# Block products for the first feed-forward matmul from chunk 7 instead of 15, accumulated in two PSUM banks

## The chip, the cores and the metric

The kernel runs on one core of a Trainium2 chip, with nothing running on the other cores. The metric is the time of one execution on the device in microseconds (us), from the first to the last instruction and what the launch adds around them. A core has five engines that each work through a queue of their own: TensorE (PE in the profile, its weight loads PEld), VectorE (DVE), ScalarE (ACT), GpSimd (POOL) and SyncE (SP), which here issues all DMAs. Matrix products land in PSUM, which has eight banks; everything else works from SBUF.

## The reference

The first half is a linear attention with random features, the second a feed-forward layer on its output:

```python
q_s, k_s = q * scale, k * scale                  # batch 8, heads 8, 576 tokens, head size 64
phi(x) = exp(x @ omega.T - |x|^2/2 - max) / sqrt(128)      # 128 features
kv  = sum over tokens of phi(k_s) * v            # per batch and head: 128 x 64
z   = sum over tokens of phi(k_s)
attn = (phi(q_s) @ kv) / (phi(q_s) @ z + 1e-6)
x = attn as 4608 tokens x 512
h = x @ w_in                                     # 512 -> 2048
g = h * tanh(softplus(h))                        # Mish
out = g @ w_out                                  # 2048 -> 512, float32
```

## The kernel before

**Precision.** Each float32 operand of a large product is split into two float16 numbers, a high part (a cast) and a low part (the rest). A product is then three TensorE products, low by high, high by low and high by high, summed in one PSUM bank.

**Chunks.** The 4608 tokens are 18 chunks of 256 (`CH`, `NCH`). A k task makes the features of two heads of one batch and its key-value sums; a q task makes the attention output `x` of 128 tokens, splits it (`x_parts`) and sends it transposed to SBUF with a DMA of SP's queue. `ff_in(c)` makes `h` of chunk c, `ff_out(c - 1)` the output of the chunk before. The main loop takes one step of `ff_in` ("i") and one of `ff_out` ("o") in turns, as the string `order` says, and between them one `step()` of an agenda in which the attention's tasks and the work put off with `later(n, ...)` (n steps later) wait for their slot. `pace(c)` sets how far ahead the attention's tasks are begun: the q tasks of a chunk start 1.6 to 2.5 chunks before its `ff_in`. The instructions are traced in this order; a scheduler then places them on the engines' queues in order of that priority as its own cost model sees them ready, and the chip follows the queues as they were placed.

**Plain chunks (2 to 14).** `ff_in(c)` takes eight steps. A step (line 676) fills one bank of the pool `ps_h` (two banks) with 24 matmuls of 256 columns; ACT then applies Mish straight from the bank (`mish`, line 821), and after every second step `g_split` (lines 72 and 83) splits the result. `ff_out` takes eight steps of 12 matmuls of 512 columns (line 845). `order` is "io" eight times.

**Block chunks (15 to 17, from `SC0` on).** `ff_in7(c)` computes the same `h` by a scheme of seven products of half-size blocks instead of eight (Winograd's form of Strassen's): `x` is cut into two halves of its columns and of its tokens, `w_in` into halves of its rows and columns, and seven products of sums of such blocks give the four blocks of `h`. Per chunk there are two groups (`gr`) of 1024 columns of `w_in`, each of seven steps of 24 matmuls of 128 columns (line 779). The sums of `w_in` that the scheme needs (s1 to s4) are made once by `s_make`, four pieces of work on DVE and ACT in chunks 11 to 14, and stored in DRAM. Each use fetches one back with two DMAs of 256 KB (`ask_sum`, line 751) into one of three places of a ring, which takes the room of blocks that are no longer needed; a load is asked for three uses ahead, behind the product that frees its place. The sums of `x` (t1 to t4) are made by `x_sums` for each chunk: four subtractions on DVE (line 548), four splits instead of two, four transposing DMAs instead of two. In this version each product gets a bank of `ps_a` (four banks, which the attention uses too): ACT copies the first into SBUF, and DVE adds every later product into SBUF (seven additions a group, line 788); Mish then reads SBUF.

In SBUF, `h` tiles (tag "ht", `HB` buffers, which `s_make` uses too), `x`'s regions 2 and 3 (tag "vf", shared with the loads of v), and split rows waiting for their transpose (tag "xs", two buffers) matter to the change.

Of the kernel before, what the change touches and what calls it, by code (L numbers as in the profile page):

```python
# [30 lines left out]
def tile_kernel(  # L31
# [19 lines left out]
    NCH = NT * P // CH  # L51
    FG = 8
    FQ = 4
    SC0 = 15
    SCALE = 1.0 / math.sqrt(math.sqrt(D))
    EPS = 1e-6 * M
    D1 = D + 1
# [30 lines left out]
    dve.memset(lnt, LNT)  # L88


    idle = const.tile([P, 512], F16, name="idle")
    dve.memset(idle, 1.0)

    def spin(n, left, right):
# [46 lines left out]

    NB = 8
    BW = KT * DF // NB
    wo_t = const.tile([P, NB, 2, BW], F16, name="wo")
    slots = [const.tile([P, 2, BW], F16, name=f"w{i}") for i in range(NB + 1)]
    slots += [wo_t[:, i] for i in range(NB)]
    def flat32(slot):
        return slot.rearrange("p a b -> p (a b)").bitcast(F32)  # L150

# [355 lines left out]
    def x_region(c, r):  # L507

        n = (4, 4, 4, 2)[r]
        if r < 2:  # L510
            return xT[c].rearrange("p a k s -> p (a k s)")[:, r * 1024:(r + 1) * 1024].rearrange(
                "p (a k s) -> p a k s", a=2, k=n
            )
        if (c, r) not in x_more:
            x_more[c, r] = sb.tile([P, 2, n, P], F16, tag="vf", name=f"xm{c}_{r}", bufs=5)
        return x_more[c, r]

    x_even = {}
# [175 lines left out]

    SUMS = ("s2", "s3", "s1", "s4")
    sums = {}

    def block(sl, a, row):  # L700
# [52 lines left out]
    def ff_in7(c):  # L753

        must(4, "x", c)
        sp = [(b_scales(b), lo, hi) for b, lo, hi in spans(c * CH, CH)]
        right = dict(b11=(0, 0), b21=(0, 2), t3=(1, 0), b22=(1, 2), t1=(2, 0), t2=(2, 2), t4=(3, 0))
        if c == SC0:
            must(4, "sums")
            for _ in range(3):  # L760
                ask_sum()

        def left(gr, op, i, a, k):
            hb, o = i // 2, k * 2 * P + i % 2 * P
            if op in SUMS:
                n = uses.index((c, gr, op))
                assert n < asked[0]
                return ring[2 * (n % 3) + hb][:, a, o:o + P]
            sl = slots[4 * gr + hb + (2 if op == "a22" else 0)]
            o += 0 if op == "a11" else BW // 2  # L770
            return sl[:, a, o:o + P]

        def products(gr, op_l, op_r):
            r, k0 = right[op_r]
            mm = [(a, y, k) for a, y in ((1, 0), (0, 1), (0, 0)) for k in range(2)]
            ph = ps_a.tile([P, FQ, P], F32, tag="a", name=f"p_{op_l}_{c}_{gr}")
            for i in range(FQ):
                for n, (a, y, k) in enumerate(mm):
                    nc.tensor.matmul(  # L779
                        out=ph[:, i, :], lhsT=left(gr, op_l, i, a, k), rhs=x_region(c, r)[:, y, k0 + k, :],  # L780
                        start=n == 0, stop=n == len(mm) - 1,
                    )
            if op_l in SUMS:
                ask_sum()
            return ph

        def add(out, in0, bank):
            dve.tensor_tensor(out=out, in0=bank, in1=in0, op=ALU.add)  # L788

        for gr in range(FT // FG):  # L790
            gT[c, gr] = sb.tile([P, 2, FG, CH], F16, tag="g", name=f"g{c}_{gr}", bufs=GB)
            h = [sb.tile([P, FQ, CH], F32, tag="ht", name=f"h{c}_{gr}_{q}", bufs=HB) for q in range(2)]
            c11, c12, c21, c22 = (x[:, :, o:o + P] for x in h for o in (0, P))


            p1 = products(gr, "a11", "b11")
            cast(act, c21, p1)
            yield
            add(c11, c21, products(gr, "a12", "b21"))
            yield  # L800
            add(c12, c21, products(gr, "s2", "t2"))
            yield
            add(c21, c12, products(gr, "s3", "t3"))
            yield
            p5 = products(gr, "s1", "t1")
            add(c22, c21, p5)
            add(c12, c12, p5)
            yield
            add(c12, c12, products(gr, "s4", "b22"))
            later(1, mish, sp, h[0], h[0])  # L810
            later(2, g_split, c, gr, 0, sp, h[0])
            yield
            add(c21, c21, products(gr, "a22", "t4"))
            later(1, mish, sp, h[1], h[1])
            later(2, g_split, c, gr, 1, sp, h[1])
            yield

    def mish(sp, h, ph):

# [57 lines left out]
        nc.sync.dma_start(out=out[row:row + P, :], in_=o)  # L877


    GB, HB, QB = 4, 5, 1  # L880
    w_dma = nc.sync

    FIRST = (0, 1, 2, 3, 4, 4, 9, 9, 19, 21, 24, 27, 32, 36, 43, 58, 59, 68)
# [45 lines left out]
    def later(after, fn, *args):  # L929
        def gen():  # L930
            fn(*args)
            yield 0
        start(gen(), after)
# [93 lines left out]
        at(slot[0] + 16 * (SC0 - 6) + 2 + 11 * i, lambda i=i: start(s_make(i // 2, i % 2)))  # L1027
    for c in range(2, NCH):
        fi, fo = (ff_in if c < SC0 else ff_in7)(c), ff_out(c - 1)
        order = "io" * 8 if c < SC0 else "iioiioioioi" * 2  # L1030
        for j, what in enumerate(order):
            if j % 2 == 0 and given[0] < min(pace(c + j / len(order)), len(items)):
                give()
            next(fi if what == "i" else fo, None)
            if (j + 1) * 16 // len(order) > j * 16 // len(order):
                step()
        for gen in (fi, fo):
            next(gen, None)
# [47 lines left out]
```

## Time and profile before

| | us |
|---|---|
| median of the runs shown | 969.31 |
| lowest run | 968.18 |
| span of the profiled execution (first to last instruction) | 965.3 |
| PE busy in it | 947.3 |
| ACT busy | 633.5 |
| DVE busy | 624.4 |
| POOL busy | 224.0 |

No time is listed for the profiled execution beside its span; the median of the runs is 4.0 us above that span. Matmuls are pipelined, so a mean duration in the list of groups (380 ns for a matmul of 512 columns) is longer than the step from one matmul to the next; the chain of work and the timeline show how long a run of matmuls takes. A line such as L72 or L83 is that of a helper (`cast`, `rest`) and serves many tiles; the names of the tiles tell which. The chunks are not marked in the trace. Their borders are read off PE's timeline, where a plain chunk is eight runs of 24 matmuls of line 676: chunk 3 starts at 225.3 us, chunk 7 at 422.4, chunk 12 at 667.3, chunk 14 at 771.3, chunk 15 at 820.9, and the last product of chunk 17 ends at 941.0.

### The profile page before, as it was taken

How to read it: one execution, taken by the hardware profiler on the slowest of the kernel's cores; microseconds unless marked ns; L12 is line 12 of the kernel's file. 1: busy time of each engine (PE TensorE's matmuls, PEld its weight loads, DVE VectorE, ACT ScalarE, POOL GpSimd, SP SyncE). 2: the span in 40 equal slices, each digit the busy share in tenths (PEclk: the TensorE clock that was granted, in tenths of full speed). 3: DMA queues.
4: the chain of work that ended last, by engine and by line, in shares of the span. 5: the costliest groups of instructions: out<-in, count | busy, mean ns of one | idle time of the engine just before them, and what ended most of it. 6: DMA issues, size and time to landing. Idle time of an engine off the chain costs nothing. (4 is left out here: it accounts for less than half of the span.)

```text
span 965.3 us, 20405 instructions
## 1 busy us (share of the span) xinstructions
PE 947.3 (98%) x8616; PEld 681.2 (71%) x8616; DVE 624.4 (65%) x1080; ACT 633.5 (66%) x818; POOL 224.0 (23%) x141
## 2 busy tenths in 40 slices
PE   9999989999999999999999999999999999999998
PEld 6788874677777777777777776777766776777773
DVE  5879797596675666656464665788889647633330
ACT  4658875687787777778667775778676866332231
POOL 0000052243233322332233333222231322200000
PEclk9989999999999999999999999999999999999999
DMA  9766324431541445313432263323552155833410
GB/s 290 265 210 205 108 50 91 102 76 54 115 104 39 113 79 117 59 59 78 97 68 60 73 119 64 89 81 74 134 122 72 34 101 102 181 116 123 141 56 33
DMA packets 142411, 100.24 MB, mean 104 GB/s; under 512 B 108656, under 2 KB 121072, under 8 KB 142320
## 3 DMA queue, kind: packets, MB, share of 16 engines
q1 hardware_dynamic: 142320, 98.95, 40.3%
q8 instruction: 67, 1.10, 0.5%
q14 instruction: 24, 0.20, 0.1%
HBM read 58.95 MB, written 13.63 MB: 75 GB/s over the span
## 5 line engine op out<-in xcount | busy, mean ns | idle before, releaser
L845 PE MATMUL po<-wo,g 128*128 128x512 f16 x1632 | 375.0, 380 | 0.0
L676 PE MATMUL ph<-xT,w 128*128 128x256 f16 (+1 forms) x2816 | 345.6, 279 | 0.7 <-ACT xT L72 0.7
L676 PEld LDWEIGHTS <-w 128*128 128x128 f16 x2688 | 261.8, 98 | 48.2 <-issue 0.7
L845 PEld LDWEIGHTS <-g 128*128 128x128 f16 x1632 | 155.1, 98 | 163.9 <-issue 2.0
L83 DVE SCALAR_TENSOR_TENSOR g<-h,us,g 128x1024 f16<-128x1024 f32 (+3 forms) x92 | 118.4, 1298 | 38.0 <-ACT g L72 37.5
L821 ACT ACTIVATE h<-ph,us 128x512 f32<-128x512 f32 (+3 forms) x152 | 83.2, 572 | 80.8 <-PE ph L676 80.1
L81 POOL TENSOR_TENSOR sq<-fq,sq 64x1024 f16<-64x1024 f32 x31 | 69.6, 2245 | 164.7 <-issue 69.0
L81 POOL TENSOR_TENSOR sk<-fk,sk 64x1152 f16<-64x1152 f32 x24 | 60.6, 2523 | 109.1 <-issue 26.3
L81 POOL TENSOR_TENSOR xs<-x,xs 128x512 f16<-128x512 f32 (+1 forms) x35 | 45.3, 1294 | 157.6 <-DVE xs L74 69.7
L72 ACT ACTIVATE g<-h,us 128x1024 f16<-128x1024 f32 (+3 forms) x80 | 72.6, 932 | 1.2
L821 ACT ACT_TABLE_LOAD x55 | 70.6, 1283 | 1.0
L354 ACT ACT_TABLE_LOAD x53 | 68.0, 1283 | 1.0
L339 DVE TENSOR_REDUCE mxq<-pq 128x4 f32<-128x512 f32 x72 | 46.8, 683 | 33.7 <-PE pq L330 33.7
L81 DVE TENSOR_TENSOR qn<-eq,qn 128x1024 f16<-128x1024 f32 x31 | 39.0, 1257 | 37.2 <-ACT qn L72 37.2
L779 PEld LDWEIGHTS <-w 128*128 128x128 f16 x1008 | 58.4, 98 | 5.9
L339 DVE TENSOR_REDUCE mxk<-pk 128x4 f32<-128x512 f32 (+1 forms) x96 | 50.2, 549 | 17.5 <-PE pk L330 17.5
L821 ACT ACTIVATE h<-h,us 128x1024 f32<-128x1024 f32 (+2 forms) x16 | 14.7, 933 | 61.6 <-DVE h L788 61.6
L354 ACT ACTIVATE eq<-eq,lnt 128x1024 f32<-128x1024 f32 x31 | 35.6, 1148 | 27.3 <-DVE eq L348 27.0
L72 ACT ACTIVATE o<-po,us 128x512 f32<-128x512 f32 (+1 forms) x38 | 25.8, 679 | 40.8 <-PE po L845 40.8
L788 DVE TENSOR_TENSOR h<-p_s,h 128x512 f32<-128x512 f32 x30 | 20.2, 689 | 42.8 <-PE p_s L779 42.8
L81 DVE TENSOR_TENSOR kp<-ek,kp 128x1152 f16<-128x1152 f32 x24 | 34.8, 1449 | 19.8 <-ACT kp L72 19.8
L81 POOL TENSOR_TENSOR vb<-vf,vb 128x640 f16<-128x640 f32 x24 | 38.9, 1621 | 34.5 <-DVE vb L74 29.7
(140 smaller groups left out, 1166.7 us busy)
## 6 DMA issues: line engine op xcount, KB each, us to landing
w<-ds SPq DMA_DIRECT2D x48, 256.0 KB, 3.4
vf<-in_vL_dram SPq DMA_DIRECT2D x32, 325.0 KB, 3.3
fk<-in_kT_dram SPq DMA_DIRECT2D x32, 288.0 KB, 3.7
fq<-in_qT_dram SPq DMA_DIRECT2D x36, 256.0 KB, 3.5
out_dram<-o SPq DMA_DIRECT2D x36, 256.0 KB, 2.3
raw<-in_w_out_dram SPq DMA_DIRECT2D x5, 1024.0 KB, 8.7
wo<-in_w_in_dram SPq DMA_DIRECT2D x4, 1024.0 KB, 13.0
raw<-in_w_in_dram SPq DMA_DIRECT2D x4, 1024.0 KB, 15.1
```

The source lines that it names most:

```text
L72: act.activation(out, in_, AF.Copy, scale=scale)
L81: eng.tensor_tensor(out=out, in0=in_, in1=hi, op=ALU.subtract)
L83: eng.scalar_tensor_tensor(out=out, in0=in_, scalar=scale, in1=hi, op0=ALU.mult, op1=ALU.subtract)
L339: sub = dve.tensor_reduce(out=mx[:, lo:hi], in_=pp[:, :m, :], axis=AX.X, op=ALU.max, negate=by_act)
L354: last = act.activation(e, e, AF.Exp, bias=lnt)
L676: nc.tensor.matmul(out=ph[:, i, :], lhsT=wi(a, k, f) if c else wi0(k, f), rhs=xT[c][:, y, k, :] if c else xT0()[:, k, :], start=n == 0, st ...
L779: nc.tensor.matmul(out=ph[:, i, :], lhsT=left(gr, op_l, i, a, k), rhs=x_region(c, r)[:, y, k0 + k, :], start=n == 0, stop=n == len(mm) - 1,)
L788: dve.tensor_tensor(out=out, in0=bank, in1=in0, op=ALU.add)
L821: act.activation(h[:, :, lo:hi], ph[:, :, lo:hi], AF.Mish, scale=us[:, 0:1])
L845: nc.tensor.matmul(out=po[i], lhsT=gT[c, gr][:, a, f % FG, i * P:(i + 1) * P], rhs=wo(y, f), start=f == 0 and (a, y) == parts[0], stop=f = ...
```

## The change

`SC0` goes from 15 to 7: chunks 7 to 14 are computed by `ff_in7` too, and the slots in which `s_make` is started, counted from `SC0`, move from chunks 11 to 14 to chunks 3 to 6. In `ff_in7` TensorE itself accumulates products: the bank `pa` gets a11·b11, then s2·t2, s3·t3 and a22·t4 on top of it, and the bank `pd` s1·t1, then s4·b22; both come from `ps_h`. After each of the first three stages of `pa` ACT copies the bank out (to c11, c12, c22), and TensorE goes on in it afterwards. The product a12·b21 has a bank of `ps_a` (`pb`). DVE adds three times a group instead of seven. The last block stays in `pa`, from where the new `mish7` reads it, traced in the same step as the last product; the Mish of the other half follows a step later. The order of the seven products changes (s1 before s3, a22 before s4), and so do the order of the sums in the ring and the last letters of `order`. Region 2 of `x` gets two buffers of its own and region 3 one (`bufs=4 - r`). `HB` goes from 5 to 4, and the constant tile `idle`, used by the first matmuls of the program, takes room of a weight slot that is filled later.

```diff
-    SC0 = 15
+    SC0 = 7
...
-    idle = const.tile([P, 512], F16, name="idle")
+    idle = slots[NB][:, 0, 0:512]
...
-            x_more[c, r] = sb.tile([P, 2, n, P], F16, tag="vf", name=f"xm{c}_{r}", bufs=5)
+            x_more[c, r] = sb.tile([P, 2, n, P], F16, tag=f"xm{r}", name=f"xm{c}_{r}", bufs=4 - r)
...
-    SUMS = ("s2", "s3", "s1", "s4")
+    SUMS = ("s2", "s1", "s3", "s4")
...
-        def products(gr, op_l, op_r):
+        def products(bank, gr, op_l, op_r, first):
...
-                        start=n == 0, stop=n == len(mm) - 1,
+                        start=first and i == 0 and n == 0, stop=n == len(mm) - 1, skip_group_check=True,
...
-            p1 = products(gr, "a11", "b11")
-            cast(act, c21, p1)
+            pa = bank(ps_h, "h", f"pa{c}_{gr}")
+            products(pa, gr, "a11", "b11", True)
+            cast(act, c11, pa)
             yield
-            add(c11, c21, products(gr, "a12", "b21"))
+            pb = bank(ps_a, "a", f"pb{c}_{gr}")
+            products(pb, gr, "a12", "b21", True)
+            add(c11, pb)
             yield
-            add(c12, c21, products(gr, "s2", "t2"))
+            products(pa, gr, "s2", "t2", False)
+            cast(act, c12, pa)
             yield
-            add(c21, c12, products(gr, "s3", "t3"))
+            pd = bank(ps_h, "h", f"pd{c}_{gr}")
+            products(pd, gr, "s1", "t1", True)
             yield
-            p5 = products(gr, "s1", "t1")
-            add(c22, c21, p5)
-            add(c12, c12, p5)
+            products(pa, gr, "s3", "t3", False)
+            cast(act, c22, pa)
+            add(c22, pd)
             yield
-            add(c12, c12, products(gr, "s4", "b22"))
+            products(pa, gr, "a22", "t4", False)
+            yield
+            products(pd, gr, "s4", "b22", False)
+            add(c12, pd)
+            later(0, mish7, sp, h[1], pa)
+            later(1, g_split, c, gr, 1, sp, h[1])
             later(1, mish, sp, h[0], h[0])
             later(2, g_split, c, gr, 0, sp, h[0])
             yield
-            add(c21, c21, products(gr, "a22", "t4"))
-            later(1, mish, sp, h[1], h[1])
-            later(2, g_split, c, gr, 1, sp, h[1])
-            yield
+
+    def mish7(sp, h, pa):
+
+        for us, lo, hi in sp:
+            if lo < P:
+                e = min(hi, P)
+                act.activation(h[:, :, lo:e], pa[:, :, lo:e], AF.Mish, scale=us[:, 0:1])
+            if hi > P:
+                b = max(lo, P)
+                act.activation(h[:, :, b:hi], h[:, :, b:hi], AF.Mish, scale=us[:, 0:1])
...
-    GB, HB, QB = 4, 5, 1
+    GB, HB, QB = 4, 4, 1
...
-        order = "io" * 8 if c < SC0 else "iioiioioioi" * 2
+        order = "io" * 8 if c < SC0 else "iioiioioiio" * 2
```

More of the change, by code (lines that the diff above doesn't have):

```diff
@@ L88, in tile_kernel @@
     dve.memset(lnt, LNT)
-    idle = const.tile([P, 512], F16, name="idle")
+    NB = 8
+    BW = KT * DF // NB
+    wo_t = const.tile([P, NB, 2, BW], F16, name="wo")
+    slots = [const.tile([P, 2, BW], F16, name=f"w{i}") for i in range(NB + 1)]
+    slots += [wo_t[:, i] for i in range(NB)]
+    idle = slots[NB][:, 0, 0:512]
     dve.memset(idle, 1.0)
@@ L136, in pow2 @@
         return top_over(p, tag, top)
[L144 to L148, printed above, removed]
     def flat32(slot):
@@ L771, in left @@
             return sl[:, a, o:o + P]
-        def products(gr, op_l, op_r):
+        def products(bank, gr, op_l, op_r, first):
             r, k0 = right[op_r]
             mm = [(a, y, k) for a, y in ((1, 0), (0, 1), (0, 0)) for k in range(2)]
-            ph = ps_a.tile([P, FQ, P], F32, tag="a", name=f"p_{op_l}_{c}_{gr}")
             for i in range(FQ):
@@ L779, in products @@
                     nc.tensor.matmul(
-                        out=ph[:, i, :], lhsT=left(gr, op_l, i, a, k), rhs=x_region(c, r)[:, y, k0 + k, :],
-                        start=n == 0, stop=n == len(mm) - 1,
+                        out=bank[:, i, :], lhsT=left(gr, op_l, i, a, k), rhs=x_region(c, r)[:, y, k0 + k, :],
+                        start=first and i == 0 and n == 0, stop=n == len(mm) - 1, skip_group_check=True,
                     )
@@ L784, in products, with bank, add @@
                 ask_sum()
-            return ph
-        def add(out, in0, bank):
-            dve.tensor_tensor(out=out, in0=bank, in1=in0, op=ALU.add)
+        def bank(pool_, tag, name):
+            return pool_.tile([P, FQ, P], F32, tag=tag, name=name)
+        def add(out, bank):
+            dve.tensor_tensor(out=out, in0=bank, in1=out, op=ALU.add)
         for gr in range(FT // FG):
```

## The prediction

> **What bounds the kernel now.** I read the page's busy times and slices first, then the busy times in windows cut at the chunks' borders, the chain of waits, and the timelines of PE and ACT.
>
> ```profile
> span 965.3 us, 20405 instructions
> PE 947.3 (98%) x8616; PEld 681.2 (71%) x8616; DVE 624.4 (65%) x1080; ACT 633.5 (66%) x818; POOL 224.0 (23%) x141
> ```
>
> TensorE is busy for 98% of the span; no other engine passes 66%. The windows, one chunk each (chunks 3, 7, 11, 12 and 15), show where the other engines come near.
>
> ```profile
> 225.28:273.73 48.45, 48.45 (x456) 34.95 (x455) 31.22 (x63) 36.51 (x39) 15.38 (x9) 1.00 0.43 94
> 422.35:471.35 49.00, 49.00 (x465) 35.30 (x464) 30.01 (x50) 38.34 (x42) 16.52 (x10) 1.00 0.36 92
> 617.23:667.34 50.11, 50.11 (x486) 36.01 (x485) 43.34 (x71) 38.37 (x55) 16.23 (x10) 1.00 0.24 70
> 667.34:719.93 52.59, 50.47 (x453) 35.35 (x452) 49.25 (x81) 39.06 (x45) 14.76 (x8) 0.97 0.54 124
> 820.85:862.00 41.15, 41.15 (x485) 29.83 (x484) 22.69 (x45) 15.09 (x22) 5.20 (x5) 1.00 0.68 165
> ```
>
> The columns are the window, its length, then busy us of PE, PEld, DVE, ACT and POOL, the granted clock, the DMA share and GB/s. In chunk 7 PE does not idle at all, with DVE at 30.0 of 49.0 us and ACT at 38.3. Chunk 12, with `s_make` in it, has DVE at 49.3 of 52.6 and loses PE time. The chain of waits then says what a step costs while TensorE is the bound:
>
> ```profile
> 814.91 2.62 PE ph L676 x24
> 817.53 0.89 PE pq L330 x16
> 818.42 2.59 PE po L845 x12
> ...
> 832.30 1.34 PE p_s L779 x24
> ...
> 940.95 20.73 PE po L845 x96
> ```
>
> A plain "i" step takes 2.62 us, a block step 1.34, an "o" step 2.59. From 821 us to the end PE alone makes the chain, but for the last copy. So a saved matmul is a saved time, unless TensorE starts to wait. Before that point, nine windows of 52 us from 200 us on (the first and the last) have no idle PE:
>
> ```profile
> 200.00:252.00 52.00, 52.00 (x528) 37.90 (x527) 37.29 (x65) 38.67 (x47) 20.43 (x11) 1.00 0.37 84
> ...
> 616.00:668.00 52.00, 52.00 (x498) 37.12 (x497) 45.19 (x73) 40.23 (x56) 16.89 (x10) 1.00 0.23 69
> ```
>
> Then it waits three times, in chunks 12, 13 and 14:
>
> ```profile
> 709.25 0.85 PE L330 MATMUL pk<-om,sk 128*128 128x128 f16 x8 [2.12 <-DVE x L498]
> 709.89 4.25 PE L845 MATMUL po<-wo,g 128*128 128x512 f16 x12
> ...
> 745.42 1.13 PE L432 MATMUL pkv<-vb,kp 128*128 128x65 f16 x30 [1.05 <-DVE kp L81]
> ...
> 811.40 0.92 PE L482 MATMUL pn<-kv,qp 128*128 128x65 f16 x24 [1.67 <-DMA qp<-qn]
> 812.15 2.75 PE L845 MATMUL po<-wo,g 128*128 128x512 f16 x12
> ```
>
> Behind the idle 2.12 us the next 12 matmuls took 4.25 us, where the same run took 2.75 behind the idle 1.67: a wait of some two microseconds costs 1.50 us more, in a lowered clock (0.97 in that chunk's window). The Trainium skill ("TensorE: Matmul & The Clock Gate", section "Why this matters for your kernels") puts that point at idle gaps above about 3 us. The trace has it lower, by 2.12, and decides.
>
> **The change, part by part.** *Matmuls.* A plain chunk has 8 steps of 2.62 = 20.96 us, a block chunk 14 of 1.34 = 18.76. That is 2.20 a chunk and 17.6 us over chunks 7 to 14, all on the path. Chunks 15 to 17 keep their number of matmuls, so nothing there.
>
> *`s_make` moved.* It leaves chunks 11 to 14; the waits of 2.12 + 1.50 and 1.05 us, both for DVE, go with it: -4.7. The third wait, for a DMA behind a late q tile, belongs to `x_sums` and stays. Its DVE work comes into chunks 3 to 6, with its eight casts for DRAM on ACT and the stores on SP's queue. Chunk 3 has 31.2 of 48.5 us on DVE already, and chunk 12's row shows where this leads: 49.3. I price it as the same waits, +4.7, from 0 (chunk 11, 43.3 us on DVE, has no wait) to twice that.
>
> *ACT and DVE in chunks 7 to 14.*
>
> ```profile
> L821 ACT ACTIVATE h<-ph,us 128x512 f32<-128x512 f32 (+3 forms) x152 | 83.2, 572 | 80.8 <-PE ph L676 80.1
> L821 ACT ACT_TABLE_LOAD x55 | 70.6, 1283 | 1.0
> L788 DVE TENSOR_TENSOR h<-p_s,h 128x512 f32<-128x512 f32 x30 | 20.2, 689 | 42.8 <-PE p_s L779 42.8
> L72 ACT ACTIVATE h<-p_a 128x512 f32<-128x512 f32 x6 | 3.5, 582 | 0.0
> L548 DVE TENSOR_TENSOR tt<-x,tt 128x256 f32<-128x256 f32 x3 | 1.3, 425 | 0.1
> L74 DVE CAST xs<-tt 128x512 f16<-128x512 f32 x3 | 1.3, 421 | 0.0
> L81 POOL TENSOR_TENSOR xs<-tt,xs 128x512 f16<-128x512 f32 x3 | 3.7, 1217 | 0.0
> ```
>
> A chunk gains six copies on ACT, 6 × 0.58 = 3.5 us, and Mish in fewer, larger pieces is about what its eight of 0.57 were. ACT comes to 38.3 + 3.5 = 41.8 of the 46.8 us that 49.0 - 2.2 leaves. DVE gains six additions, 6 × 0.69 = 4.1, and four subtractions, 4 × 0.43 = 1.7, with two more casts of 0.42 or less: some 36.5 of 46.8. POOL gains two splits, about 2 us. No engine passes TensorE, but ACT comes to 89%, and now TensorE waits for it in a new way. Each next product into `pa` must wait until ACT has copied the last. What lies between as cover: for c11, a12 and an "o" step, 1.34 + 2.59 = 3.93 us; for c12, s1 and an "o", 3.93; for c22, only an "o", 2.59; for `mish7`, s4 and an "o", 3.93, and it may need a table load of 1.28 first. A plain bank has two banks' worth, 2.59 + 2.62 + 2.59 = 7.80. Behind a waiting product everything of TensorE's queue waits, the attention's matmuls included. How late ACT is now shows for chunk 7's eight banks; the first, the worst and the last:
>
> ```profile
> 422.35 2.78 PE L676 MATMUL ph<-xT,w 128*128 128x256 f16 x24
> 429.76 2.78 PE L676 MATMUL ph<-xT,w 128*128 128x256 f16 x24
> 465.40 2.78 PE L676 MATMUL ph<-xT,w 128*128 128x256 f16 x24
> ```
>
> ```profile
> 426.55 0.69 ACT L821 ACTIVATE h<-ph,us 128x512 f32<-128x512 f32 x1
> ...
> 432.64 1.26 ACT L354 ACTIVATE ek<-ek,lnt 128x1152 f32<-128x1152 f32 x1 [3.17 <-DVE ek L348]
> ...
> 436.42 0.69 ACT L821 ACTIVATE h<-ph,us 128x512 f32<-128x512 f32 x1
> ...
> 469.08 0.69 ACT L821 ACTIVATE h<-ph,us 128x512 f32<-128x512 f32 x1
> ```
>
> From the end of the run (start + 2.62) to the end of the Mish: 2.27, 4.73 and 1.75 us; the other five lie between 0.89 and 1.66. The late one stood behind an exponential that itself waited 3.17 us for DVE. With one in eight at 4.73: c11 and c12 outlast their cover by 0.80, `mish7` with its table load by 2.08, c22 by 2.14. The attention adds 49.0 - 8 × (2.62 + 2.59) = 7.3 us a chunk, 0.33 on each of 22 steps, which widens a cover of two steps by 0.66 and of one by 0.33; left are 0.14, 1.42 and 1.81. Over 16 groups: 32/8 × 0.14 + 16/8 × 1.42 + 16/8 × 1.81 = 7.0 us. DVE's addition to c22, which s4 waits for, follows the same late copy, for which a22 has then waited already: nothing more. The bounds are 0 (every copy in time; a wait cannot gain) and, if all 16 c22 copies were as late as the worst, 29.
>
> *DMAs and `x`.*
>
> ```profile
> w<-ds SPq DMA_DIRECT2D x48, 256.0 KB, 3.4
> SPq L751 <- PE p_s L779: 52.0, 15, 9.3
> SPq L297 <- POOL sq L81: 185.3, 29, 17.7
> ```
>
> Eight chunks bring 8 × 16 = 128 more ring loads (4.2 MB a chunk, some 90 GB/s on chunk 7's 92) and 16 more transposes, all on SP's queue. There a ring load waits for TensorE (up to 9.3 us), with the attention's loads and transposes behind it, and waits itself behind loads that wait for POOL. The shortest lead of a ring load, from s2 to s4, is three block steps and two "o", 9.2 us, against 3.4 to land. Chunk 15 ran 165 GB/s beside the last q tasks without a wait. Region 3 of `x`, with one buffer, cannot be sent before the former chunk's last a22 is done, and holds one of two "xs" buffers meanwhile; it is needed 18.4 us later, so no wait of its own. The one wait like this is the 1.67 us for `qp`, in the three chunks of `x_sums`: 0 to 8 × 1.67 = 13.4, and I take 2.
>
> *Edits at nothing.* `HB` 4: a group holds two tiles, and the group before has let go of its two when the next but one begins. `idle` in a weight slot: its matmuls are the program's first. The tail: after the last product the first group's "o" steps, half of the last 20.73, cover the last Mish and its split.
>
> The sum: 965.3 - 17.6 - 4.7 + 4.7 + 7.0 + 2.0 = 956.7 of span; with the 4.0 between the span and the median of the runs, 960.7, say 960.
>
> **Rivals.** *All covered.* For it: not one wait of TensorE from 200 to 668 us, and the scheduler may place other matmuls into a gap. Only the removed matmuls and waits count: 969.3 - 17.6 - 4.7 = 947. Against it is the late copy in chunk 7. 0.14.
>
> *The waits eat the gain.* ACT at 89% answers later than in chunk 7: if each of the 16 groups waits 1.1 us at c22 or `mish7`, 17.6 us, the time is about 969. For it: ACT's queue is in order and holds exponentials that wait for DVE, which gets busier too. 0.18.
>
> *Slower, by the clock.* If a wait in a group reaches 2.1 us, it costs 2.12 + 1.50 = 3.62 with the lowered clock. In all 16 groups that is 58 us: 969.3 - 17.6 + 58 = 1010. It passes 2% from 11 groups on. It decides where ACT ends the c22 copy 2.59 + 2.1 = 4.7 us after the product: the worst lag of chunk 7. Against it, that is one in eight now. 0.08. By the 3 us of the Trainium skill's page on TensorE no clock would be lost, and the same waits would give 986.
>
> *Short matmuls don't run at half the time.*
>
> ```profile
> L779 PEld LDWEIGHTS <-w 128*128 128x128 f16 x1008 | 58.4, 98 | 5.9
> ```
>
> If each of the 336 block matmuls of a chunk took as long as its weight load, 98 ns instead of 1.34/24 = 56, a chunk would gain 14 us and the time be 969.3 - 17.6 + 113 = 1065. The rows of chunks 15 to 17 exclude it but for the attention's share in the queue: 0.01. The Trainium skill ("TensorE: Matmul & The Clock Gate", section "Back-to-back issue gap") speaks for this: it gives 81 ns for a sustained stream of loads and matmuls at 128 columns, which would make about 1019 as an estimate. The trace's 56 ns, with a load before each matmul, disagrees.
>
> **The numbers.** The forecast's own case has 0.59, from 950 to 966. Predicted is 960; the range 946 to 980 takes in "all covered", most of "eat the gain", and the bounds of `s_make` and of the transposes, and leaves out the slow cases. A difference of 2% is about what a measurement of this kernel can tell from none: 949.9 and 988.7. Faster by over 2%: most of "all covered", 0.13. Slower: 0.08 + 0.01 = 0.09. Between: 0.78.
>
> **What would show it.** Line 676 should lose 8 × 192 matmuls and line 779's successor gain 8 × 336; a group of block steps in chunk 8 should read 1.34 us a step. Waits of PE for ACT's copies (c22, `mish7`) should total some 7 us, those for DVE between 225 and 400 us some 3 to 5. The forecast is wrong if PE's idle time in chunks 7 to 14 passes 20 us or stays under 2, if chunks 3 to 6 lose over 10 us, or if the clock shows 0.9 in many slices.

## The result and the profile after

The changed kernel takes 998.73 us in the median (993.84 to 1007.79) against 969.32. The ratio on record is 1.0333 (that of these two medians would be 1.0303), with a 95% interval of 1.0292 to 1.0373. That is 32 us slower, where 9 us faster was predicted and 980 was the upper end of the range. The profiled execution spans 998.9 us and took 1000.85 in all, 1.9 more than its span.

Some executions of most of these kernels take 15 to 22 us longer at a lowered granted clock and are left out of the ratios; the longest of the four here (1007.79, mean clock 0.965, the others 0.977 to 0.982) is counted but may be one of them, and without it the change would read about 30 us instead of 32, and each difference from it below nearly 3 us less.

In the text below, microseconds that stand for a variant are its ratio to the kernel before, less one, times 969: the change itself is +32.3.

The head of the page of the changed kernel:

```profile
span 998.9 us, 23147 instructions
PE 943.6 (94%) x9768; PEld 687.7 (69%) x9768; DVE 654.8 (66%) x1152; ACT 646.0 (65%) x844; POOL 238.5 (24%) x157
...
PEclk9989999999999899999999899999999999999999
...
w<-ds SPq DMA_DIRECT2D x176, 256.0 KB, 3.8
```

TensorE's busy time fell by 3.7 us only (947.3 to 943.6), its idle time rose from 18.0 to 55.3. With 17.6 us of work gone, busy time should have been 929.7; the 13.9 above it I put down to matmuls that ran in a lowered clock: the mean granted clock was 0.979, and the same 9768 matmuls took 926.3 us in an execution of another variant (without the transposes, below) whose clock was 0.996. So -17.6 + 37.3 + 13.9 = 33.6, the difference of the spans. No engine became the bound: ACT is at 65%, VectorE at 66%. Of the three 8s in the clock's line, the first (slice 3) stands in the kernel before too; the others (slices 14 and 23, about 325 to 350 and 549 to 574 us) lie where two of the longest waits are.

The work itself shrank as predicted. PE's timeline of the changed kernel in chunk 7 (start, duration, instruction):

```profile
472.37 1.50 PE L779 MATMUL pa<-xm,w 128*128 128x128 f16 x24
473.71 1.50 PE L779 MATMUL pd<-xm,w 128*128 128x128 f16 x24
475.05 0.91 PE L483 MATMUL pn<-kv,qp 128*128 128x65 f16 x24
```

From start to start a block step takes 1.34 us. What was lost, the windows show: the columns are the stretch, its length, then busy us of PE, PEld, DVE, ACT and POOL, the clock, the DMA share and GB/s. First the changed kernel (chunks 3 to 6, 7 to 10, 11 to 14, cut where TensorE begins chunks 3, 7, 11 and 15), then the kernel before in the same chunks:

```profile
226.65:437.26 210.61, 201.15 (x1887) 142.59 (x1886) 174.14 (x305) 153.77 (x189) 66.44 (x38) 0.98 0.43 105
437.26:656.39 219.13, 197.35 (x2463) 146.22 (x2462) 140.74 (x254) 144.01 (x160) 69.38 (x42) 0.96 0.64 159
656.39:853.66 197.27, 188.22 (x2401) 139.47 (x2398) 124.53 (x228) 140.70 (x165) 53.83 (x34) 0.99 0.61 150
```

```profile
225.28:422.35 197.07, 197.07 (x1887) 141.44 (x1886) 122.33 (x238) 148.89 (x175) 59.51 (x35) 1.00 0.37 81
422.35:617.23 194.88, 194.88 (x1837) 139.45 (x1836) 113.90 (x197) 139.78 (x148) 60.32 (x32) 1.00 0.36 82
617.23:820.85 203.62, 198.78 (x1870) 141.21 (x1868) 160.38 (x259) 148.36 (x185) 56.19 (x32) 0.99 0.38 90
```

Chunks 3 to 6 take 13.5 us more (210.6 for 197.1, with the same 1887 matmuls), 7 to 10 take 24.2 more, although their products are shorter (some 50 of the attention's matmuls fall there instead of in 11 to 14), and 11 to 14 take 6.4 less. PE idles 9.5 us in chunks 3 to 6, 21.8 in 7 to 10 and 9.1 in 11 to 14, where it idled 0, 0 and 4.8. Engine totals say little about it: in chunks 7 to 10 VectorE is busy for 141 of 219 us. Who was late, the waits by engine tell (releaser, total us, times, longest). PE in the changed kernel:

```profile
PE pn L483 <- DMA qp<-qn: 14.4, 9, 3.9
PE pd L779 <- DVE h L790: 7.1, 5, 4.9
PE pn L483 <- DVE ek L349: 7.0, 2, 4.7
PE pkv L433 <- DVE h L790: 3.6, 1, 3.6
PE pkv L433 <- DVE kp L81: 3.5, 1, 3.5
...
PE pa L779 <- ACT h L72: 1.8, 2, 1.6
```

The last of these rows is the wait that the prediction had given 7.0 us, for ACT's copies of `pa`; the first, for a DMA that feeds the attention, it had put at 2 more than before. The rows between are waits for VectorE. What VectorE itself waited for, in the changed kernel:

```profile
DVE h L790 <- ACT h L72: 44.5, 11, 9.1
...
DVE xs L74 <- DMA xT<-xs: 32.3, 10, 7.3
...
DVE vmx L279 <- DMA vf<-in_vL_dram: 26.2, 13, 4.1
DVE xs L74 <- DMA xm<-xs: 15.1, 4, 6.1
```

VectorE stood 47 us in front of a cast into an `xs` buffer that a transposed DMA had not yet let go. In the kernel before such waits came to 5.3 us. The other two rows do not explain the loss: the waits at `vmx` were 26.6 us before, and those of the additions for ACT's copies (6.7 us before) are longest, 55.4 us, in one of the two fastest variants below, the one without sums of `x` and ring loads. One of the waits at `xs`, in the timeline of the changed kernel (the bracket is the idle time before and its releaser):

```profile
719.92 0.29 DVE L74 CAST xs<-x 128x256 f16<-128x256 f32 x1 [4.50 <-DMA xT<-xs]
...
739.03 3.98 SPq L469 DMA_TRANSPOSE qp<-qn  x1
...
743.11 1.20 SPq L752 DMA_DIRECT2D w<-ds  x2
...
744.40 1.28 SPq L527 DMA_TRANSPOSE xT<-xs  x1
...
746.40 6.19 SPq L527 DMA_TRANSPOSE xm<-xs  x2
749.67 0.43 DVE L74 CAST xs<-tt 128x512 f16<-128x512 f32 x1 [7.26 <-DMA xT<-xs]
750.01 0.88 DVE L340 TENSOR_REDUCE mxk<-pk 128x4 f32<-128x512 f32 x2
...
750.81 0.88 DVE L349 TENSOR_TENSOR ek<-pk,mxk 128x512 f32<-128x512 f32 x2
...
751.55 0.84 PE L483 MATMUL pn<-kv,qp 128*128 128x65 f16 x12 [4.67 <-DVE ek L349]
...
752.20 3.75 PE L863 MATMUL po<-wo,g 128*128 128x512 f16 x12
```

Read it from the top. The cast at 719.92 is region 3's (128x256) of the chunk before; its transpose is the first of the two at 746.40, so that it held one of the two `xs` buffers for over 26 us. All other regions had to take turns on the second. Region 1's transpose could be issued at 744.40 only, behind a `qp` transpose and two ring loads on SP's queue. Until it had landed, region 2's cast had no buffer, and VectorE, which takes its instructions in order, stood at that cast for 7.26 us. Behind it were `mxk` and `ek` of the attention; TensorE waited for `ek` 4.67 us, and its next 12 matmuls took 3.75 instead of 2.75. The longest wait of all has the same shape with another DMA at its head:

```profile
556.64 0.34 SPq L269 DMA_DIRECT2D vf<-in_vL_dram  x1
557.08 10.31 SPq L752 DMA_DIRECT2D w<-ds  x4
...
562.65 0.82 DVE L279 TENSOR_REDUCE vmx<-vf 128x1 f32<-128x640 f32 x1 [4.08 <-DMA vf<-in_vL_dram]
563.39 0.68 DVE L790 TENSOR_TENSOR h<-pd,h 128x512 f32<-128x512 f32 x1
...
564.12 2.72 PE L779 MATMUL pd<-xT,w 128*128 128x128 f16 x24 [4.90 <-DVE h L790]
```

Here v's load took 6.0 us to land (3.3 in the median), with ring loads issued right behind it; VectorE stood at `vmx`, and the addition that frees `pd` came behind that.

### The profile page after: what moved, and what is told of

It reads as the page before. It is cut to its first block, busy times and chain, and to the rows that moved or that the text cites. A ratio compares the mean times of both kernels' runs of the same rounds, so it can differ in the third digit from the quotient of the medians.

```text
span 998.9 us, 23147 instructions
## 1 busy us (share of the span) xinstructions
PE 943.6 (94%) x9768; PEld 687.7 (69%) x9768; DVE 654.8 (66%) x1152; ACT 646.0 (65%) x844; POOL 238.5 (24%) x157
## 5 line engine op out<-in xcount | busy, mean ns | idle before, releaser
L779 PEld LDWEIGHTS <-w 128*128 128x128 f16 x3696 | 215.0, 98 | 28.4 <-issue 10.3
L677 PE MATMUL ph<-xT,w 128*128 128x256 f16 (+1 forms) x1280 | 167.9, 288 | 1.7 <-ACT h L839 1.1
L83 DVE SCALAR_TENSOR_TENSOR g<-h,us,g 128x1024 f16<-128x1024 f32 (+3 forms) x92 | 118.2, 1298 | 21.8 <-ACT g L72 21.6
L677 PEld LDWEIGHTS <-w 128*128 128x128 f16 x1152 | 112.7, 99 | 21.6 <-issue 2.1
L81 POOL TENSOR_TENSOR xs<-x,xs 128x512 f16<-128x512 f32 (+1 forms) x43 | 49.1, 1141 | 211.8 <-DVE xs L74 108.0
L72 ACT ACTIVATE h<-pa 128x512 f32<-128x512 f32 x66 | 38.9, 589 | 63.1 <-PE pa L779 62.8
L790 DVE TENSOR_TENSOR h<-pd,h 128x512 f32<-128x512 f32 x44 | 30.2, 685 | 66.2 <-ACT h L72 37.8
L779 PE MATMUL pa<-xm,w 128*128 128x128 f16 x1056 | 66.7, 220 | 1.8 <-ACT h L72 1.8
L779 PE MATMUL pa<-xT,w 128*128 128x128 f16 x1056 | 66.1, 219 | 0.0
L81 DVE TENSOR_TENSOR qn<-eq,qn 128x1024 f16<-128x1024 f32 x31 | 41.5, 1339 | 33.8 <-ACT qn L72 33.7
L340 DVE TENSOR_REDUCE mxq<-pq 128x4 f32<-128x512 f32 x72 | 46.8, 681 | 14.0 <-PE pq L331 13.9
L483 PE MATMUL pn<-kv,qp 128*128 128x65 f16 (+1 forms) x816 | 29.2, 195 | 22.2 <-DMA qp<-qn 14.4
```

Of the source, the lines that this page charges most:

```text
L72: act.activation(out, in_, AF.Copy, scale=scale)
L81: eng.tensor_tensor(out=out, in0=in_, in1=hi, op=ALU.subtract)
L83: eng.scalar_tensor_tensor(out=out, in0=in_, scalar=scale, in1=hi, op0=ALU.mult, op1=ALU.subtract)
L340: sub = dve.tensor_reduce(out=mx[:, lo:hi], in_=pp[:, :m, :], axis=AX.X, op=ALU.max, negate=by_act)
L483: nc.tensor.matmul(out=pn[lo:hi, i, :], lhsT=qp[:, a, h, lo:hi], rhs=kv[b][:, h, y, :], start=n == 0, stop=n == 2,)
L677: nc.tensor.matmul(out=ph[:, i, :], lhsT=wi(a, k, f) if c else wi0(k, f), rhs=xT[c][:, y, k, :] if c else xT0()[:, k, :], start=n == 0, st ...
```

## The experiments

Two theories were set against each other first. One: the chains' two banks couple TensorE to ACT and VectorE (the prediction's own 7 us, grown). The other: the chains are innocent, and the loss comes from what the earlier start brings along, that is `s_make` in chunks 3 to 6, the sums of `x` with their transposes, and the ring loads.

**The chains alone.**

```diff
-    SC0 = 7
+    SC0 = 15
```

> The changed kernel with the block chunks put back to 15 to 17: the chains in two banks, mish7, the order of products and the smaller buffers stay. If the chains cost by themselves (TensorE waiting for ACT's copies): above 975. If they only cost beside the attention's work, or not at all: 967 to 971.

Ratio 1.0001 (0.9989 to 1.0014). The chains in chunks 15 to 17, where the kernel before has its separate banks, cost nothing and gain nothing. From chunk 7 on they even help: with the separate banks kept (and with them that version's order of the products and of the steps) but begun at chunk 7,

```diff
-            pa = bank(ps_h, "h", f"pa{c}_{gr}")
-            products(pa, gr, "a11", "b11", True)
-            cast(act, c11, pa)
+            p1 = products(gr, "a11", "b11")
+            cast(act, c21, p1)
...
```

> The kernel before's way of the products (a bank of its own for each product, VectorE's additions between them) from chunk 7 on, with everything else as in the changed kernel (s_make in chunks 3 to 6, the same buffers for x, four 'h' buffers). If the chains neither cost nor gain (as from chunk 15 on: ratio 1.0001), it lies with the changed kernel, 990 to 1005. If the two banks held longer by the chains are behind the waits for h (7.1 + 3.6 us), it falls below 987; if the chains' fewer additions save VectorE time that was needed, it passes 1005.

the ratio is 1.0487 (1.0431 to 1.0543), +47 us. VectorE has 154 us of work there in chunks 7 to 10 instead of 141, and TensorE waits for its additions (the window of these chunks, and two rows of its waits):

```profile
435.29:656.45 221.16, 198.10 (x2464) 145.78 (x2463) 153.95 (x283) 132.22 (x135) 68.08 (x41) 0.95 0.64 157
...
PE pk L331 <- DVE h L789: 5.4, 2, 3.0
...
PE pn L483 <- DVE h L789: 4.3, 2, 2.3
```

So the first theory falls: the chains gave back 15 us (47.2 - 32.3) of what the early start costs. Where, one profile of each can only hint: chunks 7 to 10 are 2.0 us shorter with the chains and 11 to 14 are 5.5, and most of the rest lies in chunk 15, where a single late `qp` held TensorE for 5.5 us in the version with separate banks.

**`s_make` alone, in the kernel before.**

```diff
-        at(slot[0] + 16 * (SC0 - 6) + 2 + 11 * i, lambda i=i: start(s_make(i // 2, i % 2)))
+        at(slot[0] + 16 * (7 - 6) + 2 + 11 * i, lambda i=i: start(s_make(i // 2, i % 2)))
```

> The kernel before, with only the start of the four pieces of s_make moved from chunks 11 to 14 into chunks 3 to 6; the block chunks stay 15 to 17. In the changed kernel's profile TensorE waited 9.5 us between 226 and 437 us and lost some 2.5 more in the lowered clock. If s_make's work there is the cause: 969.3 - 4.7 (the waits that leave chunks 11 to 14) + 12 = about 977. If those waits come from chunk 7's sums of x and the early ring loads instead: 965 to 970.

One time of it can be compared, 974.18, some 5 us above the kernel before; it has no interval, and lies nearer to the first outcome than to the second. Its waits in chunks 3 to 6 are much like those of the changed kernel:

```profile
PE pkv L432 <- DVE kp L81: 2.8, 1, 2.8
PE pn L482 <- DVE ek L348: 2.3, 1, 2.3
PE pn L482 <- DMA qp<-qn: 2.0, 4, 0.8
PE pq L330 <- DVE eq L348: 1.5, 1, 1.5
PE ph L676 <- ACT h L821: 1.1, 1, 1.1
```

Cut at the chunks' borders, its profile (of a longer execution, but at a clock of 1.00 in all three stretches) gives 208.0 us for chunks 3 to 6 (197.1 in the kernel before), 194.9 for 7 to 10 (194.9) and 198.1 for 11 to 14 (203.6). So `s_make` by itself costs 10.9 of the 13.5 us that chunks 3 to 6 lost, and chunks 11 to 14 get 5.5 back.

**Taking out the ring loads, the sums of `x`, and both.** Without new ring loads:

```diff
-        if n < len(uses):
+        if n < 3:
```

> The changed kernel with the ring filled once and never again, so 6 ring loads instead of 176; the products read the sums that happen to lie there, so the output is not the reference's. If the ring loads are the cause (they delay the transposes of qp and the loads of v on SP's queue and on the DMA engines): the waits for qp (9.2 us in chunks 7 to 14) and those that hang on late loads of v (3.6 and 4.9) go with their clock: 976 to 986. If the buffers of x's sums or the chains are the cause: 993 to 999.

Without the sums of `x`:

```diff
...
-        tt = sb.tile([P, 2, H * D // 2], F32, tag="o", name=f"tt{c}", bufs=2)
-        for out, in0, in1 in (
...
-        for r, src in ((1, xf), (2, tt.rearrange("p a c -> p (a c)")), (3, x0[:, second])):
-            yield from x_send(nth, c, r, src)
+        yield from x_send(nth, c, 1, xf)
...
```

> The changed kernel without the sums of x: no subtractions, no splits and no transposes of regions 2 and 3 (their products read regions 0 and 1 instead, so the output is not the reference's). If the sums of x are the cause (DVE, in order, stood 35 us in chunks 7 to 14 waiting for a split buffer that a transpose still held, and 16 more transposes share the queue): 972 to 986. If the ring loads or the chains are the cause: 993 to 999.

And with both edits:

> The changed kernel without the sums of x (no subtractions, splits and transposes of regions 2 and 3; the products read regions 0 and 1 in their place) and with the ring filled once only: both of these parts of the computation are left out. If the two costs are apart (28.6 and 17.0 us), they add up and the time is 998.7 - 45.6 = 953, a gain of 16 us over the kernel before, close to the 17.6 that the shorter products should bring. If they are the same waits seen twice (ring loads and transposes late behind each other on SP), the time is 965 to 970, no lower than without the sums alone, and the move of s_make keeps what is left of the gain (5 to 10 us).

| left out | ratio, interval | us over before |
|---|---|---|
| nothing (the change) | 1.0333 (1.0292 to 1.0373) | +32.3 |
| ring loads | 1.0126 (1.0087 to 1.0165) | +12.2 |
| sums of x | 1.0018 (1.0002 to 1.0035) | +1.7 |
| both | 0.9958 (0.9930 to 0.9986) | -4.1 |

With the ring there, the sums of `x` cost 32.3 - 1.7 = 30.6 us; without it 12.2 + 4.1 = 16.3. With the sums there, the ring costs 20.1; without them 5.8. Together they cost 36.4, of which 30.6 - 16.3 = 14.3 come only where both are (the four intervals together leave some 6 us either way). I read that as two streams on one queue, each late behind the other, but leaving out a stream takes away its bytes as well as its places in the queue, so this reading is not shown. Both of the outcomes that the last expectation had written down were missed: 953 took the two costs as separate, 965 to 970 as one and the same.

What is left without both, -4.1, is the shorter matmuls' -17.6 and what goes with `s_make` from chunks 11 to 14, with the waits in chunks 3 to 6 and a few at the banks against them. Chunks 3 to 6 take 210.0 us in that kernel (197.1 before), 7 to 10 take 195.0 (194.9) and 11 to 14 take 187.4 (203.6). Its windows of chunks 3 to 6 and 7 to 10:

```profile
225.69:435.70 210.01, 201.81 (x1887) 142.34 (x1886) 169.64 (x294) 156.02 (x191) 62.53 (x35) 0.98 0.42 102
435.70:630.73 195.03, 188.83 (x2464) 141.47 (x2463) 129.72 (x228) 141.61 (x158) 60.56 (x34) 1.00 0.38 84
```

**What of the sums of `x` costs: the work or the transposes?** All subtractions, casts and splits stay; the transposes of regions 2 and 3 go:

```diff
...
-        nc.sync.dma_start_transpose(
+        if r < 2:
+          nc.sync.dma_start_transpose(
```

> The changed kernel with the sums of x made (subtractions, casts, GpSimd's splits) but the transposed DMAs of regions 2 and 3 left out; the products read other data in their place, so this part is not the reference's. If the transposes and the 'xs' buffers that they hold are what the sums cost, the time is that without the sums at all, 968 to 975. If it is VectorE's and GpSimd's work for them, it stays at 990 to 1000.

Ratio 1.0077 (1.0051 to 1.0103), +7.5, between the two outcomes expected. So of the 30.6 us 24.8 belong to the two transposes a chunk and to what waits for them, 5.8 to the work of VectorE and GpSimd.

**Which buffer is short.** Two buffers can be what holds VectorE: `xs` itself, or region 3's single buffer, behind which a transpose would hold its `xs`. Room for either comes from one of five `vf` buffers, so that this is a third variant, as their control:

```diff
-        t = sb.tile([P, 10, D1], F32, tag="vf", name=f"vf{b}_{hp}", bufs=5)
+        t = sb.tile([P, 10, D1], F32, tag="vf", name=f"vf{b}_{hp}", bufs=4)
```

> The changed kernel with four 'vf' buffers instead of five and nothing else: the control for the two runs that paid with one of them for a third 'xs' buffer (977.1 mean of its undisturbed runs) or a second buffer of region 3 (981.5). If those gains belong to 'xs' and region 3, this one gives nothing back: 993 to 1003. If they belong to v's loads, which with four buffers are asked later and further apart and stand less in front of the transposes and of VectorE's vmx (16.9 us of waits in chunks 7 to 14), it gives 976 to 984 by itself.

```diff
# besides vf
-        xs = sb.tile([P, 2, n], F16, tag="xs", name=f"xs{c}_{r}", bufs=2)
+        xs = sb.tile([P, 2, n], F16, tag="xs", name=f"xs{c}_{r}", bufs=3)
...
```

> The changed kernel with three 'xs' buffers instead of two, paid for with one of the five 'vf' buffers. Buffer theory (the sums of x cost 28.6 us because VectorE, in order, stands in front of a cast into 'xs' until a transposed DMA has landed and let a buffer go: 32.3 + 15.1 us of such waits in the changed kernel against 5.3 before): these waits fall below 15 us and the time to 975-985. Traffic theory (the three further transposes of a chunk make every small DMA land later, qp in 5.2 us instead of 4.4, and what TensorE waits for is that): VectorE's waits for xs fall, but the time stays at 992 or above. If four vf buffers are too few, TensorE waits longer for pkv and s4's bank, and the time passes 1000.

```diff
# besides vf
-            x_more[c, r] = sb.tile([P, 2, n, P], F16, tag=f"xm{r}", name=f"xm{c}_{r}", bufs=4 - r)
+            x_more[c, r] = sb.tile([P, 2, n, P], F16, tag=f"xm{r}", name=f"xm{c}_{r}", bufs=max(2, 4 - r))
```

> The changed kernel with two buffers for region 3 of x instead of one, paid for with one of the five 'vf' buffers. If region 3's transpose, which must wait until the chunk before has read its single buffer, holds an 'xs' buffer and SP's queue (the step that the prediction costed at nothing), the time falls to 980 or below. If not (SP shows only 4.7 us of waits there for TensorE's pd), it stays within 993 to 1003.

And region 3 without a buffer of its own, with five `vf`:

```diff
...
+            if r == 3:
+                x_more[c, r] = x_more[c, 2].rearrange("p a k s -> p (a k s)")[:, 0:P * 2 * n].rearrange(
+                    "p (a k s) -> p a k s", a=2, k=n)
...
```

> The changed kernel with region 3 of x written over the front of region 2's tile, so that it has no buffer of its own to wait for; all casts, subtractions, splits and transposes stay, but region 2's front values are overwritten, so that this part of the products is not the reference's. If region 3's single buffer holds an 'xs' buffer, and VectorE with it: 985 or below. If the hold is elsewhere (the landing of regions 0 and 1): 993 to 1003.

| variant | ratio, interval | us over before | VectorE's waits at `xs` for a DMA, us, in one profile |
|---|---|---|---|
| the change | 1.0333 (1.0292 to 1.0373) | +32.3 | 47.4 |
| region 3 free to go | 1.0251 (1.0207 to 1.0294) | +24.3 | 25.0 |
| four `vf` | 1.0210 (1.0158 to 1.0262) | +20.3 | 43.9 |
| four `vf`, two of region 3 | 1.0139 (1.0109 to 1.0168) | +13.5 | 24.1 |
| four `vf`, three `xs` | 1.0094 (1.0070 to 1.0119) | +9.1 | 15.7 |

The control moved too, which neither of the expectations with one `vf` buffer fewer had provided for, and by an amount that its own had not: four `vf` buffers instead of five give 12.0 us back. Beside it the third `xs` is worth 11.2 us, clear of the intervals, and region 3's buffer 6.8 (its 982.6 just missed the 980 written down), 8.0 where it was tried alone. The intervals of these last two pairs touch, and the run of region 3 alone lies at 993.6, in the outcome written down for a hold elsewhere. So I take region 3's hold to cost some 7 to 8 us, not shown to the last us; it does halve the waits at `xs`. But ending it is not enough: with two `xs` buffers for four regions the others still wait for each other's landing.

With three `xs` (and so four `vf`) and the ring filled once only, all sums still transposed:

> The changed kernel with three 'xs' buffers (four 'vf') and the ring filled once only, so that most of w_in's sums are not the right ones; all sums of x are made and transposed. If 'xs' and the ring loads together are the cause, it comes to the floor that was measured without both, 962 to 968, with every sum of x still transposed. If the transposes' own load on the DMA engines costs, a gap stays: 972 to 980.

Ratio 1.0021 (1.0003 to 1.0040), +2.0, between the two outcomes; the waits at `xs` come to 8.0 us. That is 30 of the 32 us, with what one `vf` buffer fewer gives among them: its control without the ring was not run. Against the floor without sums and ring, -4.1, a gap of 6.1 stays, about the 5.8 that the work of the sums was found to cost above.

**Is it SP's queue or the bytes?** The ring loads issued by GpSimd instead:

```diff
-                nc.sync.dma_start(out=ring[2 * (n % 3) + hb], in_=sums[gr, hb, op])
+                nc.gpsimd.dma_start(out=ring[2 * (n % 3) + hb], in_=sums[gr, hb, op])
```

> The changed kernel with the ring's 128 loads issued by GpSimd instead of by SP: same bytes, other queue. Queue theory (the ring loads cost their 17 us because SP, in order, waits at them for the product that frees the ring's place, 22.4 + 16.8 us in chunks 7 to 14, and takes 0.6 us to issue each, and the transposes and v's loads stand behind): 982 to 988, and the waits for qp fall. Traffic theory (256 KB more in flight beside the small transfers): stays at 993 to 1003. If GpSimd's own splits of x and q now stand behind its waits at the ring: 1005 or more.

Ratio 1.0706 (1.0656 to 1.0757), +68, as the third outcome had it. The trouble only changed its queue. GpSimd took 731 ns for each of the 176 loads and stood 82 us at them for `pa` and `pd` alone, with its splits of `x` and `q` behind:

```profile
L752 POOL DMA_DIRECT2D w<-ds x176 | 128.3, 731 | 99.5 <-PE pa L779 49.7 <-PE pd L779 32.6 <-DMA ds<-s 8.2
...
PE pn L483 <- DMA qp<-qn: 39.8, 14, 15.8
```

So this run does not tell queue order from bytes for SP. It shows only that these loads, with their waits for TensorE, are dearer on GpSimd's queue than on SP's.

**Which chunks.** With blocks from chunk 11 on, and `s_make` with them in chunks 7 to 10:

```diff
-    SC0 = 7
+    SC0 = 11
```

> The changed kernel with the blocks from chunk 11 instead of 7, and so s_make in chunks 7 to 10. If each further chunk by blocks costs the same (its sums of x and its ring loads, together more than its 2.2 us of shorter matmuls), half of the 31 us of the chunks is left: 979 to 987. If the loss sits in the place where s_make stands, or in chunks 7 to 10 alone, 968 to 975. In neither case does it beat the kernel before by over 2%.

1.0024 (1.0000 to 1.0048), +2.3: four chunks by blocks cost almost nothing net. With the sums left in chunks 3 to 6 beside it:

```diff
-        at(slot[0] + 16 * (SC0 - 6) + 2 + 11 * i, lambda i=i: start(s_make(i // 2, i % 2)))
+        at(slot[0] + 16 * (7 - 6) + 2 + 11 * i, lambda i=i: start(s_make(i // 2, i % 2)))
```

> The changed kernel with blocks from chunk 11 on, but w_in's sums still made in chunks 3 to 6. Against 970.2 with the sums made in chunks 7 to 10: if making them early costs more than making them late (the change's move of s_make), 974 to 978; if it costs the same wherever it stands, 968 to 972, and the rest up to 998 belongs to the blocks in chunks 7 to 10 alone.

1.0044 (1.0026 to 1.0062), +4.3: `s_make`'s place in chunks 3 to 6 or 7 to 10 is worth 1.9 us there, within the intervals. Its windows (chunks 3 to 6, 7 to 10, 11 to 14) show where its waits are and that chunks 7 to 10 have next to none:

```profile
225.25:434.61 209.36, 198.58 (x1887) 140.92 (x1886) 170.19 (x295) 156.74 (x192) 63.03 (x35) 1.00 0.40 99
434.61:629.73 195.12, 195.05 (x1837) 139.34 (x1836) 120.51 (x209) 137.40 (x146) 63.19 (x37) 1.00 0.40 90
629.73:822.83 193.10, 188.25 (x2445) 140.76 (x2444) 131.04 (x234) 145.63 (x171) 56.55 (x35) 1.00 0.62 154
```

Blocks in chunks 7 to 10 therefore make the rest, 32.3 - 4.3 = 28.0 us; against these windows the changed kernel loses 24.0 us in chunks 7 to 10 and 4.2 in 11 to 14. What stands in those chunks and not in 11 to 14: seven of v's loads are issued in chunks 7 to 10 and one later. With the last two batches' loads and maxima left out:

```diff
...
     def v_task(b):
+        if b >= 6:
+            vstate[b] = (*vstate[5][:2], one)
+            yield 1
+            return
```

> The changed kernel without the preparation of v for the last two batches (their eight loads, of which seven are issued from 442 to 577 us, and VectorE's eight maxima of them, 0.82 us each; v of the batch before is used again), so this part is not the reference's. If blocks cost so much in chunks 7 to 10 because VectorE waits for v's loads there (16.1 us) beside its waits for 'xs' (14.7 us), one hidden without the other: 975 to 984. If v has no part in it (the loss of chunks 7 to 10 comes from the sums of x and the ring alone): 990 to 1000.

One time of it can be compared, 968.95, below the forecast of either theory, and without an interval. In its profile (of a longer execution, in which chunk 7 begins at 454.4 us) chunks 7 to 10 and 11 to 14 read

```profile
454.38:653.65 199.27, 192.13 (x2463) 142.30 (x2462) 135.58 (x236) 145.88 (x163) 69.55 (x41) 0.98 0.69 164
653.65:843.97 190.32, 186.06 (x2400) 138.88 (x2397) 122.57 (x215) 138.81 (x163) 52.55 (x32) 1.00 0.59 153
```

Chunks 7 to 10 take 199.3 us there instead of 219.1, with 7.1 us of PE's idle time instead of 21.8. The reading that fits: VectorE's waits for `xs` are mostly hidden where they stand alone (chunks 11 to 14), its waits for v are hidden where they stand alone (the kernel before in chunks 7 to 10), and both in one chunk are not. One time does not show it, and the edit also takes 8 × 0.82 = 6.6 us of work from VectorE, so its size isn't v's waits alone.

**A better version.** Blocks from chunk 11, three `xs` and four `vf` buffers, and as a control the same buffers with blocks from chunk 15:

> The blocks from chunk 11 on, sums in chunks 7 to 10, with three 'xs' and four 'vf' buffers. 20.2 us came back from these buffers with blocks from chunk 7. If the waits in chunks 11 to 14 (27.4 us of VectorE's for xs, but only 4.1 us of TensorE's) still cost, 963 to 967, a little below the kernel before; if VectorE has room there and its waits cost nothing, 968 to 971; if four 'vf' buffers hold v's loads back in chunks 7 to 10, 972 or more.

> The control for the blocks from chunk 11 with three 'xs' and four 'vf' buffers, which ran in 0.9958 of the kernel before: the same buffers with blocks from chunk 15 on as before. If the gain there is the buffers' alone, this one shows it too, 963 to 966. If it is the shorter products of chunks 11 to 14 (4 times 2.2 us) that the buffers let through, this one is at 967 to 970.

The first runs in 0.9958 of the kernel before (0.9941 to 0.9976), the second in 1.0005 (0.9986 to 1.0024). So 4 us of the 8.8 that four chunks save (4 × 2.2) do arrive, and the control shows that the buffers alone give none of it. It beats both kernels, the one before by less than half a per cent, which the interval tells from none.

## Why the prediction was wrong, by its own steps

Set against the sum by chunks, nearly all of the miss lies in two places. The sum has +4.7 us for chunks 3 to 6, where 13.5 were lost. For chunks 7 to 10 it has half of the matmuls, the copies and the transposes, -8.8 + 3.5 + 1.0 = -4.3, where 24.2 were lost. For 11 to 14 it has the same with the 4.7 of `s_make` off, -9.0, and -6.4 was measured.

*Matmuls, -17.6: right.* The step takes 1.34 us, and no row suggests otherwise.

*`s_make`, +4.7 within 0 to 9.4: right mechanism, mis-sized, and beyond its bound.* Chunks 3 to 6 lose 13.5 us, 9.5 of them PE's idle time, on VectorE's `kp` and `ek` mostly, as the row of chunk 12 had suggested, the rest in slower matmuls; `s_make` moved by itself costs 10.9 there. With that the written sign that chunks 3 to 6 lose over 10 us came true. The 4.7 taken off in chunks 11 to 14 are right where `s_make` alone moves (5.5 us); in the changed kernel PE idles 9.1 there, since other waits took the place.

*TensorE waiting for ACT's copies, +7.0: wrong in the good direction.* The row reads 1.8. With blocks in the last three chunks only, the chains are free, and from chunk 7 on they save 15 us. ACT's busy share, on which "the waits eat the gain" and "slower, by the clock" were built, came to 66% in chunks 7 to 10 (144.0 of 219.1) and 71% in 11 to 14 (140.7 of 197.3), not to 89. Over the run ACT's work grew by 12.5 us where 8 × 3.5 = 28 were reckoned: with Mish in fewer, larger pieces it loads its tables 100 times instead of 114 (all groups of table loads added up), 14 × 1.283 = 18.0 us, which I had not counted.

*DMAs and `x`, +2 within 0 to 13.4: the step that failed.* The prediction said that region 3 holds one of two `xs` buffers until the former chunk's last a22 is done, and put that at nothing because region 3 "is needed 18.4 us later, so no wait of its own". That asked only when TensorE needs region 3. It did not ask who stands at the next cast into `xs`. That is VectorE, in order, with the additions that free the banks and the attention's `mxk`, `ek` and `kp` behind it. The hold was seen rightly (26 us in the wait shown), and it costs some 7 to 8 us by itself. For the rest the other regions' transposes, queued on SP behind ring loads while they hold the buffer that is left, are what the wait shown points at; how much of it is the queue and how much the bytes stays open. What is measured: the sums of `x` with their transposes cost 30.6 us and the ring 20.1, 36.4 together, and a third `xs` buffer beside its control gives 11.2 back. The range's 13.4 priced `qp` alone, at 8 × 1.67; TensorE's waits for `qp` came to 14.4 us, 9.2 of them in chunks 7 to 14, so that bound was right for the row it was made from and blind to the rest.

*The clock.* "2.12 + 1.50" was about the right size for one wait. In all, 13.9 us of TensorE's busy time went to it, and no term of the sum held it. The third rival's result, slower by over 2% through waits and the clock, came true through another engine: it had the waits at ACT's c22 copy. The test that was written down, PE idle over 20 us in chunks 7 to 14, reads 21.8 + 9.1 = 30.9; the other, waits for VectorE in chunks 3 to 6 of 3 to 5 us, reads 6.5.

*The 4.0 us from span to median* added the profiled execution's distance from the median of other executions to what lies outside the span. The latter is 1.9 us in the changed kernel; the difference of 2 us does not matter here.

*Short matmuls at 98 ns:* excluded by the row of 1.34 us for 24.

## What to carry to other kernels

When a change adds instructions that write into a rotating buffer, ask what the engine that writes does when no buffer is free, and list what is queued behind it; the data may be needed much later, while the writer stops at once, here for up to 7.3 us at a cast. Two added streams on one queue are not priced by adding their prices: here each cost 14 us more in the presence of the other. Where the bounding engine has no idle time, as in chunks 3 to 10 before, each new wait of that engine is paid in full, and some again in the clock. A wait of an engine that feeds it is paid only as far as the bounding engine then stands: VectorE's 47 us at `xs` and 26 at `vmx` stand beside 37 us of new idle time of TensorE.

## What the runs showed that I had not expected

The length of a wait alone does not say whether the clock falls. In the changed kernel TensorE idled 2.37 us twice; the 12 matmuls behind each took 2.75 us as ever:

```profile
287.90 0.55 PE L483 MATMUL pn<-kv,qp 128*128 128x65 f16 x12 [2.37 <-DVE ek L349]
288.29 2.75 PE L863 MATMUL po<-wo,g 128*128 128x512 f16 x12
```

```profile
844.15 0.92 PE L483 MATMUL pn<-kv,qp 128*128 128x65 f16 x24 [2.37 <-DMA qp<-qn]
844.90 2.75 PE L863 MATMUL po<-wo,g 128*128 128x512 f16 x12
```

In the kernel before they took 4.25 behind 2.12. An idle 2.73 us in the changed kernel was followed by 4.44. So between 2.1 and 2.7 us it went either way, and in the version with separate banks from chunk 7 on the 12 matmuls behind an idle 3.23 us still took 2.75.

Fewer `vf` buffers made the kernel 12 us faster than the change. Its profile has 10.6 us of that in chunks 7 to 10, and TensorE's waits for VectorE's `h` and `kp` fall from 14.2 to 1.9 us. I had taken it that v's loads, issued later with fewer buffers, stand less in VectorE's way; but VectorE's waits at `vmx` do not fall (29.4 us after 26.2), and TensorE's for `qp` grow (21.6 after 14.4). No run separates this from the shift of everything behind the loads, and it stays open.
